# First two token tiles normalised as a pair in a state-space layer with a gated feed-forward block

## The chip, the cores and the metric

The kernel runs on one core of a Trainium2 chip. The metric is the device time of one execution in microseconds (us); the median over several executions counts. A core has five engines that run side by side: TensorE (PE, with its weight loads PEld) does matrix products and transposes into PSUM, VectorE (DVE) and ScalarE (ACT) do elementwise work, GpSimd (POOL) small things, and SyncE (SP) issues most of the DMA transfers. ScalarE issues a few transfers as well.

## The reference

One input x of 2048 tokens by 512 features is normalised over its features (no scale or shift). The normalised x goes through two branches, and both are added to x.

```python
def _layernorm(x, axis=-1, eps=1e-5):
    m = jnp.mean(x, axis=axis, keepdims=True)
    v = jnp.var(x, axis=axis, keepdims=True)
    return (x - m) / jnp.sqrt(v + eps)

# branch A: a diagonal complex state-space layer, 512 states
Lam_bar = jnp.exp(dt * Lam)
B_bar = ((Lam_bar - 1.0) / Lam)[:, None] * Bmat
Bu = jnp.einsum("bld,pd->blp", x + 0j, B_bar)
for t in range(L):
    h = Lam_bar[None, :] * h + Bu[:, t, :]
y = 2.0 * jnp.einsum("blp,dp->bld", hseq, Cmat).real + x * Dskip[None, None, :]

# branch B: feed-forward with 1376 hidden columns
(_gelu(x @ w_gate) * (x @ w_up)) @ w_down

xn = _layernorm(x)
return x + _A_ref(xn, ...) + _B_ref(xn, ...)
```

## The kernel before

The 2048 tokens are four blocks of 512, and each block is four tiles of 128 tokens. For each block b: `LN(b)` normalises the tiles, a transpose puts features on the partitions (`XNT[b]`), `GU` does the gate and up products with GELU and the product of both, `BU` the product with B, `CHAIN` the rotation and the scans of the state-space layer on VectorE, and `DN` the down product together with the product with C, after which the result is stored. Weights stay in SBUF.

The program is a list of operations with their reads and writes. `Sched.schedule` (line 128) plans an order for each engine from durations that are written out by hand: six rounds of a forward and a backward pass, of which the shortest plan is kept. TensorE and SyncE keep the order in which the program names their operations; VectorE, ScalarE and POOL are ordered by the plan. `emit` (line 283) then adds a wait on a semaphore wherever one engine needs another's result. The argument `after` of an operation is an additional condition on the order.

The change touches the start of the program, where TensorE has no normalised tokens yet. The order of TensorE's work there is given by lines 906 to 913:

- Ten matmuls on zeros of 512 columns ("warm", line 896) run while the data is on its way.
- Tile 0 goes alone through `LN` (line 598) with `halves=True`: statistics (line 604) and their aggregation (605) on VectorE, a cast of the mean on POOL (606), the addition of eps on VectorE (608), the root on ScalarE (609), the reciprocal (616) and the normalisation in two halves of 256 columns (622) on VectorE.
- `TR0(0, "AV")` transposes the halves of tile 0 on TensorE (line 647) into two PSUM banks. ScalarE copies the first half to SBUF (654), VectorE the second (656).
- `fill(3)`: three further matmuls on zeros, of 128 columns (line 902).
- Tile 1 goes alone through `LN`. Its statistics are held until tile 0's eps addition, its aggregation until tile 0's normalisation, by `GATE["bnag"]` and `GATE["xn"]`. Its eps addition (611) and root (612) are on ScalarE. Tiles 2 and 3 go as a pair, also with 611 and 612, held until tile 1 is normalised.
- `GU_first` (line 725) starts the gate and up products of block 0 with three column groups of 128 for tile 0 alone (line 736; 24 matmuls of 128 columns). After 16 of them `TR0(1, "A")` (line 755) transposes tile 1, and ScalarE copies it. `params()` transposes the parameters of the state-space layer (line 538); VectorE copies them (540) and computes small things with them (559, 560, 542). Then the same groups for tile 1 (24 matmuls), four matmuls of 256 columns for both tiles, the transposes of tiles 2 and 3 (`TR0(2, "V")`, `TR0(3, "A")`), and matmuls of 256 columns for the rest.
- The evacuations with GELU on ScalarE (744, 746) come after the copy of tile 3; `tables_dve` (587, 589) come after the copy of tile 2.

The loads of x are four transfers of 128 KB (line 472) on SyncE's queue; the weights follow in chunks (line 468): the first gate chunk on ScalarE's queue, then the first up chunk and the second gate and up chunks on SyncE's. After them SyncE issues block 1 of x (462) and the transposing loads of B (490).

Of the kernel before, what the change touches and what calls it, by code (L numbers as in the profile page):

```python
# [9 lines left out]
ALU = mybir.AluOpType  # L10
ACTF = mybir.ActivationFunctionType
BF16, F32, I32 = dt.bfloat16, dt.float32, dt.int32
# [334 lines left out]
NT, NB, KD, KP, KF = 16, 4, 4, 4, 11  # L347
# [4 lines left out]
EPS_BF16 = 1.0013580322265625e-05  # L352
# [12 lines left out]
def build(nc, ins, out):  # L365
    with ExitStack() as es:
# [47 lines left out]
                       buf.ap[:, b, j0:j1])  # L414
        XTk = [[Buf("XT%d_%d" % (b, i), "xt", 4 * b + i, 4 * b + i + 1) for i in range(4)] for b in range(NB)]
        XT0 = XTk[0]
        XT0h = [Buf("XT0_0h%d" % i, "xt", 0.5 * i, 0.5 * (i + 1)) for i in range(2)]
        XNh = [Buf("XN0h%d" % i, "sb", XN[0].lo + 512 * i, XN[0].lo + 512 * (i + 1)) for i in range(2)]
        XTr = lambda b: XTk[b]
        WRM = A.alloc("WRM", [128], BF16)  # L420
        PROW = A.alloc("PROW", [128], BF16)
# [173 lines left out]
            t = ACT(lambda e: e.activation(COST.ap, A1.ap, ACTF.Sin, bias=HPI.ap, scale=-SIN_SCALE), d_act(2048), [A1, HPI], [COST], "cost", after=[t])  # L595
            return ACT(lambda e: e.activation(SINT.ap, F1.ap, ACTF.Sin, scale=-SIN_SCALE), d_act(2048), [F1], [SINT], "sint", after=[t])  # L596

        def LN(b, js=range(4), on_act=False, after=(), halves=False):
            j0, j1 = js[0], js[-1] + 1
            mn, sbq, qb, rq = (cols(t, b, j0, j1) for t in (MN, SBQ, QB, RQ))  # L600
            mv = Buf("MV%d_%d" % (b, j0), "sb", MVt[b][j0].lo, MVt[b][j1 - 1].hi, MV[b].ap[:, j0:j1])
            for j in js:
                tt = 4 * b + j
                V(lambda e, tt=tt: e.bn_stats(ST[tt].ap, X[tt].ap), d_dve_1x(512), [X[tt]], [ST[tt]], "bnst", after[:1])  # L604
                GATE["bnag"] = V(lambda e, tt=tt, j=j: e.bn_aggr(MVt[b][j].ap, ST[tt].ap), D_TINY, [ST[tt]], [MVt[b][j]], "bnag", after[1:])
            POOL(lambda e: e.tensor_copy(mn.ap, mv.ap[:, :, 0]), 200, [mv], [mn], "mn")
            if halves:
                GATE["bnag"] = V(lambda e: e.tensor_scalar(sbq.ap, mv.ap[:, :, 1], EPS_BF16, None, ALU.add), D_TINY, [mv], [sbq], "sbq")
                ACT(lambda e: e.activation(qb.ap, sbq.ap, ACTF.Sqrt), d_act(4), [sbq, SCR], [qb], "sqrt")
            elif on_act:  # L610
                ACT(lambda e: e.activation(sbq.ap, mv.ap[:, :, 1], ACTF.Identity, bias=EPS.ap), d_act(4), [mv, EPS, SCR], [sbq], "sbq")
                ACT(lambda e: e.activation(qb.ap, sbq.ap, ACTF.Sqrt), d_act(4), [sbq], [qb], "sqrt")
            else:
                V(lambda e: e.tensor_scalar(sbq.ap, mv.ap[:, :, 1], EPS_BF16, None, ALU.add), D_TINY, [mv], [sbq], "sbq")
                POOL(lambda e: e.tensor_tensor(qb.ap, sbq.ap, HALF.ap[:, 0:j1 - j0], ALU.pow), 1100, [sbq, HALF], [qb], "pow")
            V(lambda e: e.reciprocal(rq.ap, qb.ap), 150, [qb], [rq], "rq")
            for j in js:
                tt = 4 * b + j
                xs = XN[tt % 8]
                for c0, c1 in (((0, 256), (256, 512)) if halves else ((0, 512),)):  # L620
                    w = [XNh[c0 // 256]] if halves else [xs]
                    GATE["xn"] = V(lambda e, tt=tt, j=j, xs=xs, c0=c0, c1=c1: e.tensor_scalar(  # L622
                        xs.ap[:, c0:c1], X[tt].ap[:, c0:c1], mn.ap[:, j - j0:j - j0 + 1], rq.ap[:, j - j0:j - j0 + 1],
                        ALU.subtract, ALU.mult), 190 + 0.13 * (c1 - c0) if halves else d_dve_ts4x(512), [X[tt], mn, rq], w, "ln_n",
                                   [GATE["xn"]] if c0 else ())

        def SKIP(b):
            for tt in range(4 * b, 4 * b + 4):
# [3 lines left out]

        TBANK = []

        def TR0(j, engs):
            if not TBANK:
                TBANK.extend([next_bank(), next_bank()])
            per = KD // len(engs)
            for n, eng in enumerate(engs):
                bank = TBANK[(j + n) % 2]  # L640
                pt = PS[bank].bitcast(BF16)

                def f(e, n=n, pt=pt):
                    ins_ = None
                    for q in range(per):
                        k = per * n + q
                        ins_ = e.transpose(pt[:, 128 * q:128 * (q + 1)], XN[j].ap[:, 128 * k:128 * (k + 1)], IDN.ap)
                    return ins_
                PE(f, 75.0 * per, [XN[j] if len(engs) == 1 else XNh[n], IDN], [BANK[bank]], "T0")
                dst = XNT[0].ap[:, per * n:per * (n + 1), 128 * j:128 * (j + 1)]  # L650
                src = pt[:, 0:128 * per].rearrange("p (q t) -> p q t", q=per)
                tok = XT0[j] if len(engs) == 1 else XT0h[n]
                if eng == "A":
                    GATE["evTA"] = ACT(lambda e, src=src, dst=dst: e.activation(dst, src, ACTF.Copy), d_act(128 * per), [BANK[bank]], [tok], "evT")
                else:
                    GATE["evT"] = V(lambda e, src=src, dst=dst: e.tensor_copy(dst, src), 110 + 0.6 * 128 * per, [BANK[bank]], [tok], "evT")  # L656

        def TR(b):
            tts = list(range(4 * b, 4 * b + 4))
# [62 lines left out]
            V(lambda e: e.tensor_tensor(ssb.ap[:, :, 1, :], TB.ap[:, :, 0, :], TA.ap[:, :, 1, :], ALU.subtract),  # L722
              d_dve_tt2x(2048), [TA, TB], [SSc[k3][s][1] for s in range(KP)], "post_im")

        def GU_first(fts, early, single):
            banks = [{ft: next_bank() for ft in fts} for h in range(2)]

            def mm(ft, u, j0, j1):
                W, Wc = ((WG, WGc), (WU, WUc))[u]
                h, q0 = j0 // 2, 256 * u + 128 * (j0 % 2)  # L730
                bank = banks[h][ft]

                def f(e):
                    ins_ = None
                    for dk in range(KD):
                        ins_ = e.matmul(PS[bank][:, q0:q0 + 128 * (j1 - j0)], W.ap[:, dk, 128 * ft:128 * (ft + 1)],  # L736
                                        XNT[0].ap[:, dk, 128 * j0:128 * j1], start=(dk == 0), stop=(dk == KD - 1))
# [12 lines left out]

            for u in range(2):
                for ft in early:
                    mm(ft, u, 0, 1)
                    if single and u == 1 and ft == early[0]:
                        TR0(1, "A")
            params()
            for ft in early:
                for u in range(2):
                    mm(ft, u, 1, 2)
            late = [ft for ft in fts if ft not in early]  # L760
            mm(late[0], 0, 0, 2)
            TR0(2, "V")
            TR0(3, "A")
            for ft in early:
                evac(ft, 0, [GATE["evTA"]])
            for ft in late[1:]:
                mm(ft, 0, 0, 2)
            for ft in late:
                mm(ft, 1, 0, 2)
                evac(ft, 0)  # L770
            for ft in fts:
                for u in range(2):
                    mm(ft, u, 2, 4)
                evac(ft, 1)
# [111 lines left out]
                    for c in parts:  # L886
                        hidden(j, *c); states(j, *c); store(j, *c)

        nwarm = 10
        wrm4 = WRM.ap.unsqueeze(1).broadcast_to([128, 4, 128])  # L890
        wb = next_bank()

# [5 lines left out]
        def fill(n):  # L898
            def f(e):
                ins_ = None  # L900
                for _ in range(n):
                    ins_ = e.matmul(PS[wb][:, 0:128], WRM.ap, WRM.ap, start=True, stop=True)
                return ins_
            PE(f, 60.0 * n, [WRM], [BANK[wb]], "fill")

        PE(fwarm, d_pe([512] * nwarm) * 1.6, [WRM], [BANK[wb]], "warm")
        LN(0, [0], True, halves=True)
        TR0(0, "AV")
        fill(3)
        LN(0, [1], True, [GATE["bnag"], GATE["xn"]])  # L910
        LN(0, [2, 3], True, [GATE["xn"]])
        load_B()
        GU_first(range(5), range(3), True)
        tables_dve()
        GATE["before_gelu"] = [tables_act([GATE["last_gelu"]])]
        BU(0)
# [81 lines left out]
```

## Time and profile before

| | us |
|---|---|
| median of 4 runs | 179.85 |
| lowest and highest | 179.81 and 180.42 |
| the profiled execution | 179.85 |
| its span, first to last instruction | 178.0 |
| TensorE busy | 173.6 |
| VectorE busy | 157.8 |
| ScalarE busy | 92.3 |
| POOL busy | 10.2 |

Times in the profile are counted from the start of the span. A row of a timeline is a run of like instructions of one engine: start, length until the last one ends, engine, line of the kernel, operation, result and operand, the number of instructions, and in brackets the idle time of the engine before it with what ended it. Instructions of one engine overlap in part, so that a row can reach beyond the start of the next; the ends of matmuls are modelled.

### The profile page before, as it was taken

The numbers are of one execution on the slowest core, as the hardware profiler recorded it, in microseconds if no ns is written. First come the engines' busy times: TensorE is split into PE (matmuls) and PEld (weight loads), VectorE is DVE, ScalarE is ACT, GpSimd is POOL, SyncE is SP. The second block draws the span as 40 slices with busy tenths as digits, with TensorE's granted clock in tenths as the row PEclk, the third lists the DMA queues.
The fourth block names the chain that finished last, engine by engine and source line by source line (L and its number), as shares of the span: only waits on it lengthen the run. The fifth ranks groups of instructions, "written<-read, shape, count | busy, mean of one in ns | idle before, by whom it ended". The sixth has DMA issues, their size and how long they took to land.

```text
span 178.0 us, 2528 instructions
## 1 busy us (share of the span) xinstructions
PE 173.6 (97%) x914; PEld 86.6 (49%) x929; DVE 157.8 (89%) x277; ACT 92.3 (52%) x179; POOL 10.2 (6%) x21
## 2 busy tenths in 40 slices
PE   7999999999999999999999999999999999999994
PEld 2597464444644444444644444444464444444453
DVE  4869998997998989989999999989999999999511
ACT  3389999976677799002667793000667800710000
POOL 3020022042000000200000000000000000000000
PEclk9999999999999999999999999999999999999999
DMA  5999914989045000002014100000001000002211
GB/s 132 344 294 169 312 37 90 152 224 327 1 88 63 0 0 0 2 29 92 0 29 89 30 0 4 29 29 29 29 4 29 0 0 0 0 0 66 85 49 40
DMA packets 26387, 12.90 MB, mean 72 GB/s; under 512 B 17704, under 2 KB 26376, under 8 KB 26376
## 3 DMA queue, kind: packets, MB, share of 16 engines
q1 hardware_dynamic: 25824, 12.36, 28.5%
q10 hardware_dynamic: 552, 0.40, 0.9%
q8 instruction: 7, 0.11, 0.3%
q14 instruction: 4, 0.03, 0.1%
HBM read 6.46 MB, written 2.10 MB: 48 GB/s over the span
## 4 chain that ended last, share of the span: by engine, by line
PE 83%; ACT 5%; DVE 2%; issue 1%; ACTq 0%
PE PS L853 37%; PE PS L813 33%; PE PS L673 12%; PE PS L787 2%; ACT arena L677 2%; ACT arena L595 1%; ACT arena L596 1%; DVE arena L748 1%; DVE arena L589 1%; ACT L594 1%; DVE arena L587 0%; ACT arena L746 0%; DVE arena L871 0%; ACT arena L744 0%; ACT arena L594 0%
## 5 line engine op out<-in xcount | busy, mean ns | idle before, releaser
L853 PE MATMUL PS<-arena 128*128 128x512 bf16 (+3 forms) x317 | 65.9, 366 | 0.3
L813 PE MATMUL PS<-arena 128*128 128x512 bf16 x273 | 60.7, 379 | 0.4
L853 PEld LDWEIGHTS PS<-arena 128*128 128x128 bf16 (+1 forms) x323 | 30.8, 98 | 35.2
L828 ACT ACTIVATE arena<-PS 128x512 bf16<-128x512 f32 x35 | 21.1, 603 | 46.8 <-PE PS L813 33.5
L813 PEld LDWEIGHTS PS<-arena 128*128 128x128 bf16 x280 | 27.4, 98 | 32.1
L706 DVE TENSOR_TENSOR_SCAN arena<-arena 128x512 bf16<-128x512 f32 x32 | 39.1, 1255 | 0.9 <-POOL arena L544 0.9
L673 PE MATMUL PS<-arena 128*128 128x512 bf16 x126 | 28.0, 379 | 0.1
L831 ACT ACTIVATE arena<-PS 128x512 bf16<-128x512 f32 x35 | 21.1, 603 | 5.2 <-PE PS L813 5.1
L673 PEld LDWEIGHTS PS<-arena 128*128 128x128 bf16 x128 | 12.5, 98 | 14.9
L677 ACT ACTIVATE arena<-PS 128x512 bf16<-128x512 f32 x32 | 18.0, 597 | 2.2 <-PE PS L673 2.2
L871 DVE TENSOR_TENSOR arena<-PS,arena 128x512 bf16<-128x512 f32 (+2 forms) x17 | 10.9, 652 | 9.0 <-PE PS L853 8.9
L833 DVE TENSOR_TENSOR arena<-arena 128x512 bf16<-128x512 bf16 x35 | 13.7, 414 | 2.1 <-ACT arena L831 2.0
L845 ACT ACTIVATE PS<-arena 128x512 f32<-128x512 bf16 (+2 forms) x17 | 9.6, 581 | 5.8 <-DVE arena L871 5.1
L604 DVE BATCH_NORM_STATS2 arena<-arena 128x6 f32<-128x512 bf16 x16 | 10.3, 683 | 1.4 <-DMA arena<-in_A_x_dram 1.2
L736 PE MATMUL PS<-arena 128*128 128x256 bf16 (+1 forms) x104 | 9.5, 248 | 0.4 <-DVE arena L656 0.3
L693 DVE TENSOR_TENSOR arena<-arena 128x4096 bf16<-128x4096 bf16 (+1 forms) x5 | 9.3, 1856 | 0.0
L695 DVE TENSOR_TENSOR arena<-arena 128x4096 bf16<-128x4096 bf16 (+1 forms) x5 | 9.3, 1856 | 0.0
L718 DVE TENSOR_TENSOR arena<-arena 128x4096 bf16<-128x4096 bf16 x4 | 9.2, 2288 | 0.1
L719 DVE TENSOR_TENSOR arena<-arena 128x4096 bf16<-128x4096 bf16 x4 | 9.1, 2283 | 0.0
L736 PEld LDWEIGHTS PS<-arena 128*128 128x128 bf16 x104 | 8.1, 98 | 1.3 <-issue 0.5
L622 DVE TENSOR_SCALAR arena<-arena 128x512 bf16<-128x512 bf16 (+1 forms) x17 | 6.1, 401 | 0.4
L787 PE MATMUL PS<-arena 128*128 128x192 bf16 x64 | 5.9, 246 | 0.0
(89 smaller groups left out, 108.4 us busy)
## 6 DMA issues: line engine op xcount, KB each, us to landing
out_dram<-arena SPq DMA_DIRECT2D x15, 128.0 KB, 1.7
arena<-in_A_x_dram SPq DMA_DIRECT2D x3, 512.0 KB, 6.9
arena<-in_B_w_down_dram SPq DMA_DIRECT2D x1, 1280.0 KB, 6.5
arena<-in_A_x_dram SPq DMA_DIRECT2D x4, 128.0 KB, 2.9
arena<-in_B_w_gate_dram SPq DMA_DIRECT2D x1, 512.0 KB, 6.1
arena<-in_B_w_up_dram SPq DMA_DIRECT2D x1, 512.0 KB, 7.0
arena<-in_B_w_gate_dram SPq DMA_DIRECT2D x1, 480.0 KB, 4.2
arena<-in_B_w_up_dram SPq DMA_DIRECT2D x1, 480.0 KB, 5.9
```

What stands on the lines that cost most here:

```text
L604: V(lambda e, tt=tt: e.bn_stats(ST[tt].ap, X[tt].ap), d_dve_1x(512), [X[tt]], [ST[tt]], "bnst", after[:1])
L673: ins_ = e.matmul(PS[bank][:, :], BBT[c][dk].ap[:, 128 * s:128 * (s + 1)], XNT[b].ap[:, dk, :], start=(dk == 0), stop=(dk == KD - 1))
L677: ACT(lambda e, bank=bank, k3=k3, s=s, c=c: e.activation(SSc[k3][s][c].ap, PS[bank][:, :], ACTF.Copy), d_act(512), [BANK[bank]], [SSc[k3][ ...
L706: V(lambda e, g=g, rb=rb, init=init: e.tensor_tensor_scan(g.ap, rb, g.ap, init, ALU.mult, ALU.add), d_dve_scan(512), [g, PA[RRr]] + ([CARc ...
L736: ins_ = e.matmul(PS[bank][:, q0:q0 + 128 * (j1 - j0)], W.ap[:, dk, 128 * ft:128 * (ft + 1)], XNT[0].ap[:, dk, 128 * j0:128 * j1], start=( ...
L813: ins_ = e.matmul(PS[bank][0:m, c0:c1], W.ap[:, dk, 128 * ft:128 * ft + m], XNT[b].ap[:, dk, c0:c1], start=(dk == 0), stop=(dk == KD - 1))
L828: GATE["last_gelu"] = ACT(lambda e, bg=bg, kk=kk, m=m: e.activation(GG[kk].ap[0:m, :], PS[bg][0:m, :], ACTF.Gelu_apprx_tanh), d_act(512), ...
L831: ACT(lambda e, bu=bu, kk=kk, m=m: e.activation(UPB[kk].ap[0:m, :], PS[bu][0:m, :], ACTF.Copy), d_act(512), [BANK[bu]], [UPB[kk]], "evU")
L833: V(lambda e, kk=kk, m=m, ft=ft, k2=k2: e.tensor_tensor(HTt[k2][ft].ap[0:m, :], GG[kk].ap[0:m, :], UPB[kk].ap[0:m, :], ALU.mult), d_dve_tt ...
L845: ACT(lambda e: e.activation(PS[bank][:, c0:c1], X[tt].ap[:, c0:c1], ACTF.Copy), d_act(c1 - c0), [X[tt]], [BANK[bank]], "seed")
L853: ins_ = e.matmul(PS[bank][:, c0:c1], l_[:, 128 * j:128 * (j + 1)], r_[:, c0:c1], start=False, stop=last and n == len(ops) - 1, skip_group ...
L871: V(lambda e: e.tensor_tensor(OUTB[ko].ap[:, c0:c1], PS[bank][:, c0:c1], XD[tt].ap[:, c0:c1], ALU.add), d_dve_1x(c1 - c0), [BANK[bank], XD ...
```

## The change

Tiles 0 and 1 now go through `LN` together, in the way in which tiles 2 and 3 did: both statistics, both aggregations, one cast of the means, one eps addition, one root and one reciprocal for two columns, and then the normalisation of each tile in one instruction of 512 columns. The eps addition is on VectorE for every group (line 611 on ScalarE is gone). `TR0` transposes a whole tile into one bank, with one copy: tile 0's on VectorE, tile 1's on ScalarE. Both are transposed ahead of the first product, and the transposes of tile 1 between the products of tile 0 are gone. The conditions that held tile 1's statistics and aggregation are gone; those of tiles 2 and 3 are held until VectorE's copy of tile 0. There are eleven instead of ten warm-up matmuls and two instead of three fills. The modelled durations of the transposes and copies are other numbers too.

```diff
-        def LN(b, js=range(4), on_act=False, after=(), halves=False):
+        def LN(b, js=range(4), on_act=False, after=()):
...
-                V(lambda e, tt=tt: e.bn_stats(ST[tt].ap, X[tt].ap), d_dve_1x(512), [X[tt]], [ST[tt]], "bnst", after[:1])
-                GATE["bnag"] = V(lambda e, tt=tt, j=j: e.bn_aggr(MVt[b][j].ap, ST[tt].ap), D_TINY, [ST[tt]], [MVt[b][j]], "bnag", after[1:])
+                V(lambda e, tt=tt: e.bn_stats(ST[tt].ap, X[tt].ap), d_dve_1x(512), [X[tt]], [ST[tt]], "bnst", after)
+                V(lambda e, tt=tt, j=j: e.bn_aggr(MVt[b][j].ap, ST[tt].ap), D_TINY, [ST[tt]], [MVt[b][j]], "bnag")
             POOL(lambda e: e.tensor_copy(mn.ap, mv.ap[:, :, 0]), 200, [mv], [mn], "mn")
-            if halves:
-                GATE["bnag"] = V(lambda e: e.tensor_scalar(sbq.ap, mv.ap[:, :, 1], EPS_BF16, None, ALU.add), D_TINY, [mv], [sbq], "sbq")
+            V(lambda e: e.tensor_scalar(sbq.ap, mv.ap[:, :, 1], EPS_BF16, None, ALU.add), D_TINY, [mv], [sbq], "sbq")
+            if on_act:
                 ACT(lambda e: e.activation(qb.ap, sbq.ap, ACTF.Sqrt), d_act(4), [sbq, SCR], [qb], "sqrt")
-            elif on_act:
-                ACT(lambda e: e.activation(sbq.ap, mv.ap[:, :, 1], ACTF.Identity, bias=EPS.ap), d_act(4), [mv, EPS, SCR], [sbq], "sbq")
-                ACT(lambda e: e.activation(qb.ap, sbq.ap, ACTF.Sqrt), d_act(4), [sbq], [qb], "sqrt")
             else:
-                V(lambda e: e.tensor_scalar(sbq.ap, mv.ap[:, :, 1], EPS_BF16, None, ALU.add), D_TINY, [mv], [sbq], "sbq")
                 POOL(lambda e: e.tensor_tensor(qb.ap, sbq.ap, HALF.ap[:, 0:j1 - j0], ALU.pow), 1100, [sbq, HALF], [qb], "pow")
...
-                for c0, c1 in (((0, 256), (256, 512)) if halves else ((0, 512),)):
-                    w = [XNh[c0 // 256]] if halves else [xs]
-                    GATE["xn"] = V(lambda e, tt=tt, j=j, xs=xs, c0=c0, c1=c1: e.tensor_scalar(
...
+                V(lambda e, tt=tt, j=j, xs=xs: e.tensor_scalar(
+                    xs.ap, X[tt].ap, mn.ap[:, j - j0:j - j0 + 1], rq.ap[:, j - j0:j - j0 + 1], ALU.subtract, ALU.mult),
+                  d_dve_ts4x(512), [X[tt], mn, rq], [xs], "ln_n")
...
-        def TR0(j, engs):
+        def TR0(j, eng):
             if not TBANK:
                 TBANK.extend([next_bank(), next_bank()])
...
+            bank = TBANK[j % 2]
+            pt = PS[bank].bitcast(BF16)
+
+            def f(e):
+                ins_ = None
+                for q in range(KD):
+                    ins_ = e.transpose(pt[:, 128 * q:128 * (q + 1)], XN[j].ap[:, 128 * q:128 * (q + 1)], IDN.ap)
+                return ins_
+            PE(f, 56.0 * KD, [XN[j], IDN], [BANK[bank]], "T0")
+            dst = XNT[0].ap[:, :, 128 * j:128 * (j + 1)]
+            src = pt[:, 0:512].rearrange("p (q t) -> p q t", q=KD)
+            if eng == "A":
+                GATE["evTA"] = ACT(lambda e: e.activation(dst, src, ACTF.Copy), d_act(512), [BANK[bank]], [XT0[j]], "evT")
+            else:
+                GATE["evT"] = V(lambda e: e.tensor_copy(dst, src), 420, [BANK[bank]], [XT0[j]], "evT")
...
             for u in range(2):
                 for ft in early:
                     mm(ft, u, 0, 1)
-                    if single and u == 1 and ft == early[0]:
-                        TR0(1, "A")
             params()
...
-        nwarm = 10
+        nwarm = 11
...
-        LN(0, [0], True, halves=True)
-        TR0(0, "AV")
-        fill(3)
-        LN(0, [1], True, [GATE["bnag"], GATE["xn"]])
-        LN(0, [2, 3], True, [GATE["xn"]])
+        LN(0, [0, 1], True)
+        TR0(0, "V")
+        TR0(1, "A")
+        fill(2)
+        LN(0, [2, 3], True, [GATE["evT"]])
         load_B()
-        GU_first(range(5), range(3), True)
+        GU_first(range(5), range(3))
```

More of the change, by code (lines that the diff above doesn't have):

```diff
@@ L416, in build @@
         XT0 = XTk[0]
-        XT0h = [Buf("XT0_0h%d" % i, "xt", 0.5 * i, 0.5 * (i + 1)) for i in range(2)]
-        XNh = [Buf("XN0h%d" % i, "sb", XN[0].lo + 512 * i, XN[0].lo + 512 * (i + 1)) for i in range(2)]
         XTr = lambda b: XTk[b]
@@ L619, in LN @@
                 xs = XN[tt % 8]
-                for c0, c1 in (((0, 256), (256, 512)) if halves else ((0, 512),)):
-                    w = [XNh[c0 // 256]] if halves else [xs]
[L622 to L625, printed above, removed]
+                V(lambda e, tt=tt, j=j, xs=xs: e.tensor_scalar(
+                    xs.ap, X[tt].ap, mn.ap[:, j - j0:j - j0 + 1], rq.ap[:, j - j0:j - j0 + 1], ALU.subtract, ALU.mult),
+                  d_dve_ts4x(512), [X[tt], mn, rq], [xs], "ln_n")
         def SKIP(b):
@@ L633, in build @@
         TBANK = []
-        def TR0(j, engs):
+        def TR0(j, eng):
             if not TBANK:
                 TBANK.extend([next_bank(), next_bank()])
[L638 to L656, printed above, removed]
+            bank = TBANK[j % 2]
[12 more added lines that the diff above has]
+                GATE["evT"] = V(lambda e: e.tensor_copy(dst, src), 420, [BANK[bank]], [XT0[j]], "evT")
         def TR(b):
@@ L723, in CHAIN, with GU_first @@
               d_dve_tt2x(2048), [TA, TB], [SSc[k3][s][1] for s in range(KP)], "post_im")
-        def GU_first(fts, early, single):
+        def GU_first(fts, early):
             banks = [{ft: next_bank() for ft in fts} for h in range(2)]
```

## The prediction

> **What bounds the kernel now.** I read the page first: engine shares, then the timeline of each engine over the first 17 us, then the chain of waits and the landings of the loads.
>
> ```profile
> PE 173.6 (97%) x914; PEld 86.6 (49%) x929; DVE 157.8 (89%) x277; ACT 92.3 (52%) x179; POOL 10.2 (6%) x21
> ```
>
> TensorE (PE) is busy for 97% of the span. The share is an average, so the question is where its idle stretches lie. Its timeline (start, length, engine, line, count, idle before):
>
> ```profile
> 0.99 4.45 PE L896 MATMUL PS<-arena 128*128 128x512 bf16 x10 [0.99 <-DVE arena L516]
> 5.41 0.67 PE L647 MATMUL PS<-arena 128*128 128x128 bf16 x4
> ...
> 6.55 1.12 PE L736 MATMUL PS<-arena 128*128 128x128 bf16 x16 [0.31 <-DVE arena L656]
> 7.51 0.39 PE L647 MATMUL PS<-arena 128*128 128x128 bf16 x4
> 7.74 0.61 PE L736 MATMUL PS<-arena 128*128 128x128 bf16 x8
> 8.28 0.18 PE L538 MATMUL PS<-arena 12*128 12x12 bf16 x1
> 8.59 1.95 PE L736 MATMUL PS<-arena 128*128 128x128 bf16 x28
> 10.38 0.65 PE L647 MATMUL PS<-arena 128*128 128x128 bf16 x8
> 10.87 5.84 PE L736 MATMUL PS<-arena 128*128 128x256 bf16 x52
> ```
>
> From 8.59 on each group starts where the one before runs out, and the chain of waits is then nearly all TensorE, back to back to 175.8 us. So whatever moves the start of the 256-column matmuls (10.87) moves the end by the same amount, as long as no other engine becomes late. Ahead of it TensorE waits for the layer norm of the first tiles, on VectorE (DVE) and ScalarE (ACT):
>
> ```profile
> 2.93 0.69 DVE L604 BATCH_NORM_STATS2 arena<-arena 128x6 f32<-128x512 bf16 x1 [1.20 <-DMA arena<-in_A_x_dram]
> 3.66 0.18 DVE L605 BATCH_NORM_AGGREGATE arena<-arena 128x2 bf16<-128x6 f32 x1
> 3.87 0.16 DVE L608 TENSOR_SCALAR arena<-arena 128x1 bf16<-128x1 bf16 x1
> ...
> 5.00 0.73 DVE L622 TENSOR_SCALAR arena<-arena 128x256 bf16<-128x256 bf16 x2
> ...
> 6.11 0.29 DVE L656 COPY arena<-PS 128x256 bf16<-128x256 bf16 x1 [0.16 <-PE PS L647]
> 6.68 0.16 DVE L616 RECIPROCAL arena<-arena 128x1 f32<-128x1 bf16 x1 [0.27 <-ACT arena L612]
> 6.95 0.41 DVE L622 TENSOR_SCALAR arena<-arena 128x512 bf16<-128x512 bf16 x1
> 7.46 1.29 DVE L604 BATCH_NORM_STATS2 arena<-arena 128x6 f32<-128x512 bf16 x2
> 8.67 0.30 DVE L605 BATCH_NORM_AGGREGATE arena<-arena 128x2 bf16<-128x6 f32 x2
> ```
> ```profile
> 4.13 0.20 ACT L609 ACTIVATE arena<-arena 128x1 bf16<-128x1 bf16 x1
> 7.94 0.60 ACT L654 ACTIVATE arena<-PS 128x512 bf16<-128x512 bf16 x1 [1.29 <-PE PS L647]
> 9.00 0.29 ACT L611 ACTIVATE arena<-arena 128x2 bf16<-128x2 bf16 x1 [0.47 <-DVE arena L540]
> ```
>
> The reader is to see two waits. The first matmul (6.55) comes 0.15 us after VectorE's copy ends at 6.40. The tile-1 matmuls (8.59) come 0.05 us after ScalarE's copy of tile 1 ends at 8.54; the row of TensorE waits gives that one 0.2 us.
>
> **The change, step by step, until the first matmul.** Each offset is a difference of rows above. Statistics of tile 0 start at 2.93 as now (the loads of x are untouched). Those of tile 1 follow 0.60 later (1.29 - 0.69, from the pair at 7.46): 3.53; its data lands at about 3.4 (issue 1.2, 2.2 to landing). Aggregates: the pair at 7.46 reaches them 1.21 later, so 4.14; two take 0.30, end 4.44. The eps addition on VectorE starts 0.03 later: 4.47. Root: 0.26 after that start (3.87 to 4.13): 4.73; ScalarE is free, its first root ended at 3.99. Reciprocal 0.24 later (6.44 to 6.68): 4.97. Normalisation 0.27 later: 5.24; one whole tile 0.41, so 5.65. Transpose of tile 0: 0.06 after (5.35 to 5.41): 5.71. The eleventh warm-up matmul adds 0.43 and runs out at about 5.66, just clear of it. A whole transposed tile reaches its copy 0.42 after its first transpose (10.38 to 10.80). I add 0.05, because the warm-up runs at 0.43 us per 512 columns while later matmuls take 0.216: TensorE is at half pace until about 5.8, in the middle of these transposes. Copy on VectorE from 6.18, 0.42 for 512 columns (the row at 10.80): 6.60. First matmul 0.05 to 0.15 later, by the two waits above; I take the middle, **6.70, 0.15 later than now**. That is what the halves were worth.
>
> **From there to 10.87.** Now 6.55 to 8.59 is 2.04 us: 24 matmuls at 0.056 (24 of 128 columns and 4 of 256 take 1.79 from 8.59 to 10.38; four at 0.109 leave 1.35), that is 1.34; four transposes 0.22; the other 0.48 is the parameter transpose and waits, the one on tile 1's copy foremost. Afterwards tile 1 is transposed ahead of the first matmul (normalised 5.57 to 5.98, copied by ScalarE 0.60 from about 6.46 to 7.06), so its transposes and its wait are both gone from this stretch: 6.70 + 1.34 = 8.04; parameter transpose 0.15 (0.09 gap as now at 8.19 to 8.28, and 0.06); 8.19 + 1.79 = 9.98 for the transposes of tile 2, now 10.38. **Shift: -0.40 us.** A fill fewer (0.056) lies in idle time before the first matmul.
>
> Tiles 2 and 3 must be ready by 9.98. Their statistics are held until the copy of tile 0 ends (6.60); by the offsets above normalisation starts 2.31 after the statistics: 6.64 + 2.31 = 8.95, ended 9.36, at most 0.3 more if the parameter operations (0.13, 0.18, 0.15) fall between: 9.7, still 0.25 ahead. The tile-1 matmuls until 9.98 are the work that hides this chain; whatever of it goes beyond is paid in full. The new condition (statistics of tile 2 after tile 0's copy) makes VectorE wait for no other engine, as the copy is its own; queued behind are the parameter copies, which only the tables after 11 us need. ScalarE loses two eps additions (0.29 each) and one root (0.20), POOL one cast (0.19), VectorE one reciprocal (0.16): all in idle time of those engines, costed at nothing. No DMA moves on any queue, SP's and POOL's included.
>
> What TensorE meets sooner: the up weights for tile 0 land at 7.24 (2.64 + 4.6), wanted at 7.37; the second gate chunk at 9.22 (3.12 + 6.1), wanted 9.53; the second up chunk at 10.67 (3.67 + 7.0), wanted at about 10.9; the transposed B at 15.4 (4.87 + 10.5), wanted near 16.1. All fit, the up chunk with 0.2 to spare. ScalarE's copy of tile 3 (11.07), its GELU table load (11.68) and the evacuations follow the same transposes, so they move along.
>
> Bounds. Upper: if tile 0's aggregate goes before tile 1's statistics, 0.2 more; with 0.05 for the handoff the shift is -0.15. Lower: handoff 0.05 and no half pace, -0.5.
>
> **A rule on the clock.** The row shows the pace doubling between 4.80 and 5.8. The Trainium skill ("TensorE: Matmul & The Clock Gate", Part 1: The HAM clock gate) says the clock is released after a window of some 3.4 us of activity that runs free of the kernel, so the point varies by about half a microsecond from run to run. By the row the sum is -0.40; by a release half a microsecond later, at 6.3, an estimate from that page's figure is some 0.2 us less gain, as only the transposes would be slow.
>
> **The sum.** The profiled execution took 179.85 us (span 178.0 and 1.85 around it), equal to the median of the runs. 179.85 - 0.40 = 179.45, with 179.35 to 179.70 from the bounds.
>
> **Rivals.**
> (1) *A transfer takes the shift back.* The second up chunk has 0.2 us to spare. For: it is the tightest landing, and this is one execution. Against: its issue at 3.67 depends on nothing that moves. If it lands 0.2 to 0.4 later than in the trace, 0 to 0.2 of the shift is lost at first and all of it at 0.6: 179.65 to 179.85.
> (2) *Slower: the order is planned anew and VectorE becomes late at the end.* The planner orders VectorE and ScalarE for the whole kernel from its own durations. VectorE is 99% busy from 120 to 160 us (39.71 of 40) and ends the last chain at 160.4; TensorE wants it after 142.7 + 76 x 0.216 + 11 x 0.216 = 161.5. That is 1.1 us of slack, and one badly placed operation costs that order already: VectorE waits 0.90 us for POOL at 41.2. The point is 1.1 us of new VectorE idle; two more such waits, 1.8, make TensorE wait 0.7, three 1.6: with the shift, 180.15 to 181.05, middle 180.6. Against: in the planner's durations tile 1's matmuls start at the same place in both, so little below them has cause to move.
> (3) *The clock is released late.* Against: eleven warm-up matmuls keep TensorE as busy as before. Deciding point: each microsecond of half pace after 6.70 costs 0.5; slower than now from a release at 7.5, 180.1 at 8.0.
> (4) *More is gained.* TensorE has no idle left after 10.87 to win, so over 0.54 us needs the first matmul at or before 6.55: only with an unforeseen handoff.
>
> **Numbers.** A measurement of this kernel tells 0.3% (0.54 us) from no change: below 179.31 or above 180.39. Forecast 0.52; (1) 0.12; (2) 0.24; (3) 0.05; (4) 0.07. Faster takes (4) and 0.04 of the forecast: 0.11. Slower takes most of (2), some of (3), and 0.04 for orders that I can't see: 0.26. The same: 0.63. The range leaves out (4)'s far end and the upper part of (2): 179.1 to 180.6.
>
> **What would show it.** Right: first 128-column matmul near 6.70, no transposes between 6.7 and 8, no wait at the tile-1 matmuls, transposes of tile 2 near 9.98, 256-column matmuls near 10.47, and a stream without holes to about 175.4. Wrong: tile-2 transposes waiting for VectorE, the up weights at line 736 waiting for a DMA, or any TensorE gap over 0.3 us after 11 us, above all at line 853 near 161.

## The result and the profile after

The changed kernel takes 179.58 us (median of 33 runs, 179.36 to 180.02); the kernel before 179.84 (median of 53 runs, 179.66 to 180.42). The ratio is 0.9986 with a 95% interval of 0.9981 to 0.9991: a gain of 0.14%, real but inside the 0.3% that the prediction called no change. The forecast was 179.45 us, a shift of -0.40.

The profiled execution of the changed kernel took 180.25 us, 0.67 above the median. Where these 0.67 us went is also what the change is about. First the engine shares, then VectorE's timeline (start, length, engine, line, operation, count, idle before it):

```profile
PE 172.7 (97%) x914; PEld 86.5 (48%) x929; DVE 156.7 (88%) x276; ACT 92.0 (52%) x175; POOL 10.0 (6%) x20
```
```profile
2.92 0.69 DVE L602 BATCH_NORM_STATS2 arena<-arena 128x6 f32<-128x512 bf16 x1 [1.22 <-DMA arena<-in_A_x_dram]
4.04 0.69 DVE L602 BATCH_NORM_STATS2 arena<-arena 128x6 f32<-128x512 bf16 x1 [0.43 <-DMA arena<-in_A_x_dram]
4.65 0.30 DVE L603 BATCH_NORM_AGGREGATE arena<-arena 128x2 bf16<-128x6 f32 x2
4.99 0.17 DVE L605 TENSOR_SCALAR arena<-arena 128x2 bf16<-128x2 bf16 x1
...
5.77 0.74 DVE L614 TENSOR_SCALAR arena<-arena 128x512 bf16<-128x512 bf16 x2
6.67 0.42 DVE L643 COPY arena<-PS 128x512 bf16<-128x512 bf16 x1 [0.17 <-PE PS L635]
```

The second statistics row waits 0.43 us for the load of x: tile 1 landed at 4.0 instead of 3.4, and the whole pair, tile 0 with it, is normalised that much later (5.77, forecast 5.24). TensorE in the same execution:

```profile
6.24 0.72 PE L635 MATMUL PS<-arena 128*128 128x128 bf16 x8 [1.42 <-DVE arena L614]
6.80 0.28 PE L887 MATMUL PS<-arena 128*128 128x128 bf16 x2
7.25 1.50 PE L723 MATMUL PS<-arena 128*128 128x128 bf16 x24 [0.17 <-DVE arena L643]
8.68 0.18 PE L536 MATMUL PS<-arena 12*128 12x12 bf16 x1
8.79 1.95 PE L723 MATMUL PS<-arena 128*128 128x128 bf16 x28
10.57 0.61 PE L635 MATMUL PS<-arena 128*128 128x128 bf16 x8
11.02 5.84 PE L723 MATMUL PS<-arena 128*128 128x256 bf16 x52
```

The wait that the change was to remove is gone: after the parameter transpose at 8.68 TensorE goes on at 8.79, where the kernel before, after its one at 8.28, went on only at 8.59. The first matmul comes at 7.25 instead of 6.55, the 256-column matmuls at 11.02 instead of 10.87. Later in this execution TensorE has one more hole, ahead of the first B product of block 1:

```profile
26.86 6.85 PE L798 MATMUL PS<-arena 128*128 128x512 bf16 x31
33.78 6.42 PE L660 MATMUL PS<-arena 128*128 128x512 bf16 x28
```

A matmul of 512 columns takes 0.216; the first of these starts at 26.65 by the pace (its record is missing), and 32 of them end at 33.56. So 0.22 us are lost. Two of the transposing transfers of block 1, issued at 27.7 and 29.0:

```profile
L648 SPq DMA_TRANSPOSE arena<-arena x2: 1264/1264/1265, 27.7 to 29.0; - x2
...
DMA to landing us min/median/max: 2.5/3.5/4.5
```

One took the usual 2.5 us, the other 4.5: issued at 29.0, it landed at about 33.5, just ahead of the matmul that needs it.

Two explanations lay open. Theory A: the start gains what was computed, and loses again what the input data lands late. Theory B: the planner has made a new order for VectorE and ScalarE over the whole kernel (the two kernels' lists differ from the parameter operations on), and this order makes the hole at 33.6 in every execution.

### The profile page after: what moved, and what is told of

Read it like the earlier page. It is cut to its first block, busy times and chain, and to the rows that moved or that the text cites. A ratio compares the mean times of both kernels' runs of the same rounds, so it can differ in the third digit from the quotient of the medians.

```text
span 178.4 us, 2519 instructions
## 1 busy us (share of the span) xinstructions
PE 172.7 (97%) x914; PEld 86.5 (48%) x929; DVE 156.7 (88%) x276; ACT 92.0 (52%) x175; POOL 10.0 (6%) x20
## 4 chain that ended last, share of the span: by engine, by line
PE 94%; DMA 2%; DVE 1%; issue 1%; SPq 0%; ACT 0%; DVEq 0%; ACTq 0%
PE PS L838 37%; PE PS L798 34%; PE PS L660 16%; PE PS L723 5%; PE PS L772 3%; DMA arena<-in_A_x_dram 2%; PE PS L635 0%; DVE arena L602 0%; DVE arena L643 0%; DVE arena L614 0%; SPq L470 0%; DVE arena L856 0%; DVE arena L603 0%; ACT arena L607 0%; DVE arena L605 0%
## 5 line engine op out<-in xcount | busy, mean ns | idle before, releaser
L813 ACT ACTIVATE arena<-PS 128x512 bf16<-128x512 f32 x35 | 20.9, 599 | 43.4 <-PE PS L798 33.1
L816 ACT ACTIVATE arena<-PS 128x512 bf16<-128x512 f32 x35 | 20.8, 598 | 5.6 <-PE PS L798 5.4
L664 ACT ACTIVATE arena<-PS 128x512 bf16<-128x512 f32 x32 | 17.9, 600 | 3.6 <-PE PS L660 3.5
L614 DVE TENSOR_SCALAR arena<-arena 128x512 bf16<-128x512 bf16 x16 | 5.7, 404 | 0.3
```

Of the source, the lines that this page charges most:

```text
L664: ACT(lambda e, bank=bank, k3=k3, s=s, c=c: e.activation(SSc[k3][s][c].ap, PS[bank][:, :], ACTF.Copy), d_act(512), [BANK[bank]], [SSc[k3][ ...
L813: GATE["last_gelu"] = ACT(lambda e, bg=bg, kk=kk, m=m: e.activation(GG[kk].ap[0:m, :], PS[bg][0:m, :], ACTF.Gelu_apprx_tanh), d_act(512), ...
L816: ACT(lambda e, bu=bu, kk=kk, m=m: e.activation(UPB[kk].ap[0:m, :], PS[bu][0:m, :], ACTF.Copy), d_act(512), [BANK[bu]], [UPB[kk]], "evU")
```

## Experiments

The ratio given with a time is that to the kernel before, run beside it on the same chip (its median was 179.78 to 179.82 us there), with its 95% interval; it is not always the quotient of the two medians.

Where the planner would have made yet another order, an explicit one is put in its place after planning, in this manner (the lists hold the numbers of the operations):

```diff
         S.schedule()
+        for e_, ids in ORDER.items():
...
+            S.order[e_] = [S.ops[i] for i in ids]
         S.emit()
```

### The changed kernel again: after_again and after_third

No edit.

> The changed kernel once more, for a second profiled execution. Its first one took 180.25 us where the median of its runs is 179.58; in it the statistics of tile 1 started at 4.04 (0.43 us of waiting for x) and TensorE had a hole of 0.22 us at 33.6 before the first B product of block 1. Theory A (landing): the front end gains 0.40 us when tile 1's data is there, and the pair pays one for one for what it lands later than 3.5; expected here: statistics of tile 1 at 3.53 to 4.05, the first 128-column matmul 3.2 us after that start, time near 179.45 plus the lateness. Theory B (order): the newly planned order of VectorE and ScalarE makes the hole at 33.6 in every execution and costs 0.15 to 0.22 us; expected: the hole again, and x on time.

> The changed kernel a third time, on the same chip as the three others, for the comparison and for one more profile of the landings. Theory A: each profile's start of the 256-column matmuls is 10.47 plus what tile 1 lands beyond 3.53 plus any wait for the up chunk, within 0.1; no hole near 33.6 unless a transposing transfer lands late; median 179.45 to 179.80.

Measured: 179.78 us (179.36 to 180.10), ratio 0.9994 (0.9984 to 1.0003), and 179.52 (179.42 to 180.07), ratio 0.9990 (0.9980 to 0.9999). The profile of after_third is the undisturbed case, VectorE and TensorE:

```profile
2.96 1.29 DVE L602 BATCH_NORM_STATS2 arena<-arena 128x6 f32<-128x512 bf16 x2 [1.26 <-DMA arena<-in_A_x_dram]
...
6.19 0.42 DVE L643 COPY arena<-PS 128x512 bf16<-128x512 bf16 x1 [0.17 <-PE PS L635]
```
```profile
6.76 1.51 PE L723 MATMUL PS<-arena 128*128 128x128 bf16 x24 [0.17 <-DVE arena L643]
8.20 0.18 PE L536 MATMUL PS<-arena 12*128 12x12 bf16 x1
8.31 1.95 PE L723 MATMUL PS<-arena 128*128 128x128 bf16 x28
10.10 0.61 PE L635 MATMUL PS<-arena 128*128 128x128 bf16 x8
10.54 1.69 PE L723 MATMUL PS<-arena 128*128 128x256 bf16 x14
```

Both tiles' statistics run in one go, the second from 3.56 (2.96 + 1.29 - 0.69); the first matmul is at 6.76 (forecast 6.70), tile 2's transposes at 10.10 (9.98), the 256-column matmuls at 10.54 (10.47). That execution took 179.52 us. In after_again the data of tile 1 was on time too, but not the first up chunk:

```profile
6.64 0.83 PE L723 MATMUL PS<-arena 128*128 128x128 bf16 x12 [0.17 <-DVE arena L643]
7.89 0.84 PE L723 MATMUL PS<-arena 128*128 128x128 bf16 x12 [0.41 <-DMA arena<-in_B_w_up_dram]
...
11.01 1.26 PE L723 MATMUL PS<-arena 128*128 128x256 bf16 x10
```

The gate matmuls (12 at 0.056) are through at 7.31 and the next starts at 7.89: 0.58 us lost, the gain of the change and more, and the execution took 179.99. In neither profile is there a hole near 33.6. The hole that theory B took for a constant one was there in one execution, with one late transfer.

### Start and order taken apart: old_order and new_order

The changed kernel's start with the rest in the order of the kernel before, and the reverse; the lists are joined at the parameter copy on VectorE, the first evacuation on ScalarE and the exponential on POOL.

> The changed kernel's start, but from the parameter copy on VectorE, the first evacuation on ScalarE and the exponential on POOL the order in which the kernel before has them. Theory A (landing): like the changed kernel, 179.58 within 0.1. Theory B (order): the hole at 33.6 goes, 179.36 to 179.43.

> The reverse: the kernel before with its own start, and from the same places on the order that the changed kernel has. Theory A (landing): like the kernel before, 179.84 within 0.1. Theory B (order): 0.15 to 0.22 slower than it, 180.0 to 180.06, with a hole near 33.4.

Measured: old_order 179.65 us, ratio 0.9985 (0.9976 to 0.9993); new_order 179.84, ratio 1.0002 (0.9991 to 1.0013). So the start carries the difference, with the old order as with the new (0.9994 for after_again on the same chip; the intervals overlap). That the new order costs nothing doesn't follow from the median of new_order, whose interval reaches up to 0.23 us; it follows from the profiles. That of new_order has no hole near 34.3, where its first B product of block 1 stands, and from the start of the 256-column matmuls on both orders take the same time within 0.05 us (see the sums below). So theory B falls. One thing is left of it: the four transposing transfers of block 1 begin 14.0 to 14.5 us after the first 256-column matmul with the new order (eleven profiles), and 13.8 after it with the old one (three). A late transfer has less room there, and in the first execution the order may have had a share in the hole.

Two rows of old_order's TensorE show the start once more with a tile 1 that is a quarter of a microsecond late (statistics at 3.78):

```profile
6.99 1.50 PE L753 MATMUL PS<-arena 128*128 128x128 bf16 x24 [0.17 <-DVE arena L673]
...
10.76 0.49 PE L753 MATMUL PS<-arena 128*128 128x256 bf16 x3
```

The profiled execution of new_order took 180.75 us. It shows that the old start is open to late weights as well:

```profile
7.12 0.84 PE L766 MATMUL PS<-arena 128*128 128x128 bf16 x12 [0.83 <-DMA arena<-in_B_w_gate_dram]
8.21 0.40 PE L766 MATMUL PS<-arena 128*128 128x128 bf16 x4 [0.25 <-DMA arena<-in_B_w_up_dram]
```

### One part undone: t1_middle

```diff
                 for ft in early:
                     mm(ft, u, 0, 1)
+                    if u == 1 and ft == early[0]:
+                        TR0(1, "A")
...
         TR0(0, "V")
-        TR0(1, "A")
         fill(2)
```

> The changed kernel with one part undone: tile 1 is transposed after 16 of tile 0's matmuls, as before, with the changed kernel's order on the other engines. By the prediction's steps the first matmul stays at 6.70, the transposes of tile 1 come at 7.60, ScalarE's copy ends at 8.62, the tile-1 matmuls start at 8.67 and the transposes of tile 2 at 10.46: 0.08 behind the kernel before, 179.9. So the pair by itself costs a little, and moving the transposes of tile 1 is what gains. If the gain came from the pair or the eps addition instead, it would stay near 179.6.

Measured: 180.08 us (179.84 to 180.33), ratio 1.0004 (0.9994 to 1.0015). The gain is gone, as expected: the pair with its whole tiles doesn't gain by itself, the place of tile 1's transposes does. TensorE:

```profile
6.88 1.05 PE L753 MATMUL PS<-arena 128*128 128x128 bf16 x16 [0.50 <-DVE arena L673]
7.78 0.39 PE L665 MATMUL PS<-arena 128*128 128x128 bf16 x4
8.00 0.61 PE L753 MATMUL PS<-arena 128*128 128x128 bf16 x8
8.54 0.18 PE L566 MATMUL PS<-arena 12*128 12x12 bf16 x1
8.85 1.95 PE L753 MATMUL PS<-arena 128*128 128x128 bf16 x28
...
11.08 0.38 PE L753 MATMUL PS<-arena 128*128 128x256 bf16 x2
```

The transposes stand among tile 0's products again, and so does the wait for their copy (8.54 to 8.85, where after_third goes from 8.20 to 8.31). From the first matmul to the 256-column ones it takes 4.20 us, in after_third 3.78. Tile 1's statistics started at 3.63 in this execution; without these 0.10 us the 256-column matmuls would stand at 10.98, 0.11 behind the kernel before, where 0.08 was expected. The eleventh warm-up matmul, the fill and the eps addition were not undone one by one; this run has them all as in the changed kernel and gains nothing.

### Landings moved: x1_first, gate_later, x1_third and x1_third_before

x1_first gives tile 1's load the first place on ScalarE's queue (the gate chunk second):

```diff
-            S.dma(lambda e, j=j: e.dma_start(X[j].ap, ...), 128 * 1024, writes=[X[j]], tag="ld_x0")
+            S.dma(lambda e, j=j: e.dma_start(X[j].ap, ...), 128 * 1024, writes=[X[j]], tag="ld_x0", queue="scalar" if j == 1 else "sync")
```

> The changed kernel in its own order, with tile 1's load as the first one on ScalarE's queue (0.74 instead of 1.17 on SyncE's), and the first gate chunk right behind it. Theory A (landing): tile 1 is there by 3.5 in nearly all executions, statistics of tile 1 at 3.53, first 128-column matmul near 6.7, median 179.43 to 179.50 and a narrower spread. Theory B (order): like the changed kernel, 179.58, with the hole at 33.6.

Measured: 179.91 us (179.72 to 180.00), ratio 1.0002 (0.9993 to 1.0011). A miss, and an instructive one. VectorE's first rows:

```profile
3.34 1.28 DVE L636 BATCH_NORM_STATS2 arena<-arena 128x6 f32<-128x512 bf16 x2 [1.64 <-DMA arena<-in_A_x_dram]
```

Tile 1 landed at 3.5 as wanted, but tile 0, loading at the same moment, came at 3.3 instead of 2.9. The statistics of tile 1 then follow at 3.93, and the first matmul at 7.13. The spread is narrow and the gain is lost: both theories failed on the median, and A only by its guess that tile 0 would not mind.

gate_later issues the first gate chunk after the three parameter loads on ScalarE's queue (an edit of the order alone).

> The changed kernel in its own order, with the first gate chunk issued on ScalarE's queue after all three parameter loads, about 0.4 us later. Theory A (landing, in the form the last runs left): what lands beside x sets when tile 1's last piece comes (3.42 to 4.16 in five profiles, the gate chunk issued at 1.59); with the gate chunk out of the way tile 1 lands by 3.5, median 179.45 to 179.50. The gate chunk itself then lands near 6.1, wanted at 6.7. If the lateness of tile 1 has nothing to do with the gate chunk: like the changed kernel, 179.58 to 179.78.

Measured: 180.06 us (179.62 to 180.50), ratio 1.0007 (0.9996 to 1.0019). Also a miss: in its profile the statistics of tile 1 start at 3.61, so this one profile gives no sign that the gate chunk makes tile 1 late, though it can't rule it out. The up chunk was late in it, as in after_again:

```profile
7.92 0.84 PE L753 MATMUL PS<-arena 128*128 128x128 bf16 x12 [0.27 <-DMA arena<-in_B_w_up_dram]
```

Whether the later gate chunk makes the up chunk late more often isn't shown by one profile; a median of 180.06 and a lowest time of 179.62 would fit it.

What makes the last piece of tile 1 late in some executions stays open. That its lateness is paid was tried directly, by exchanging the loads of tile 1 and tile 2 in both kernels (the edit in words; it stands in the explicit order of SyncE):

```diff
-SyncE: x tile 0, x tile 1, x tile 2, x tile 3, ...
+SyncE: x tile 0, x tile 2, x tile 1, x tile 3, ...
```

> The changed kernel in its own order with the loads of tile 1 and tile 2 in exchanged places on SyncE's queue, so that tile 1 lands where tile 2 did, at L = 5.3 to 5.8. Theory A (landing): the pair pays every microsecond beyond 3.53, that is L - 3.53; at L = 5.5 it is 179.45 + 1.97 = 181.4, slower than the kernel before with the same exchange (next run) by 0.2. If the pair did not hang on tile 1's landing: below 180.

> The kernel before in its own order with the same exchange. Tile 1's statistics stand ahead of tile 0's reciprocal in VectorE's order, but start only at 4.14, so it pays what tile 1 lands beyond that, L - 4.14; at L = 5.5: 179.85 + 1.36 = 181.2. So the sign of the change flips: here the kernel before is ahead by 0.2. If the change's gain has nothing to do with the landing, the changed kernel stays ahead by 0.2 to 0.4.

Measured: 183.57 us (ratio 1.0200, 1.0178 to 1.0223) for the changed start and 181.70 (1.0103, 1.0074 to 1.0133) for the old one. The statistics of tile 1 start at 5.54 and 5.57 in the two profiles, so the landing is the same in both, and the sign of the change flips as expected. But the changed start is behind by 1.87 instead of 0.2. In x1_third the rows of TensorE say why:

```profile
8.95 2.72 PE L757 MATMUL PS<-arena 128*128 128x128 bf16 x24
11.60 0.19 PE L570 MATMUL PS<-arena 12*128 12x12 bf16 x1
11.72 2.95 PE L757 MATMUL PS<-arena 128*128 128x128 bf16 x28
...
14.95 1.25 PE L757 MATMUL PS<-arena 128*128 128x256 bf16 x10
```

24 matmuls take 2.72 us instead of 1.50: 0.107 each, half pace. The next 28 take 2.95 instead of 1.95. The first matmul at 8.95 is 0.2 later than the 8.74 that the statistics at 5.54 give (5.54 + 3.20, see the sums below), as tile 0's transposes ran at half pace too, and half pace, until about 13.9 by the spacing of the matmuls, costs the rest. The kernel before lost less to the clock (see the last section). So most of the 1.87 us is the clock's, and the flip of the medians alone wouldn't prove the landing. The rows do:

```profile
5.57 0.69 DVE L638 BATCH_NORM_STATS2 arena<-arena 128x6 f32<-128x512 bf16 x1 [1.53 <-DMA arena<-in_A_x_dram]
```
```profile
7.98 1.86 PE L770 MATMUL PS<-arena 128*128 128x128 bf16 x16 [0.31 <-DVE arena L690]
```

In x1_third_before the first product comes 2.41 us after tile 1's statistics, as in the kernel before (4.14 to 6.55); in x1_third 3.41 after them, 3.20 and the slow transposes. Each start pays what tile 1 lands late, from 4.14 and from 3.53 on.

### The clock: no_warm

```diff
-        nwarm = 11
+        nwarm = 1
```

> The changed kernel in its own order with one warm-up matmul instead of eleven. This prices the third rival, the clock of TensorE: if the pace rises only after some 3.4 to 4.8 us of activity, which then starts at 5.7, the first stretch runs at half pace until 9 to 10.5 and the kernel takes 1.3 to 2.0 us longer, 180.9 to 181.6, with tile-0 matmuls 0.107 apart. If the pace does not depend on the warm-up: like the changed kernel, 179.6.

Measured: 181.14 us (180.81 to 181.93), ratio 1.0077 (1.0050 to 1.0104). The data was on time; what is slow is TensorE:

```profile
6.95 2.57 PE L753 MATMUL PS<-arena 128*128 128x128 bf16 x24
9.56 1.95 PE L753 MATMUL PS<-arena 128*128 128x128 bf16 x28
...
11.80 1.47 PE L753 MATMUL PS<-arena 128*128 128x256 bf16 x12
```

Tile 0's products run at 0.107, and from 9.23 on, by the trace's clock record, at full pace (28 in 1.95 again). Half pace has the price that was expected for it. The change doesn't call it up: the eight profiles with ten or eleven warm-up matmuls and x's loads in their place that have a clock record show the release of the clock between 4.2 and 6.0, ahead of the first product. Three others with eleven warm-up matmuls have no record, and there the spacing of the matmuls has to tell: full pace from about 3.7 in after and x1_first, but only from about 6.7 in gate_first.

### Versions that may beat both: gate_first and split_copy

gate_first wants the up chunk 0.7 us later by doing the gate products of both tiles first:

```diff
             for u in range(2):
                 for ft in early:
                     mm(ft, u, 0, 1)
-            params()
-            for ft in early:
-                for u in range(2):
+                if u == 0:
+                    params()
+                for ft in early:
                     mm(ft, u, 1, 2)
```

> The changed kernel in its own order on the other engines, but TensorE does the gate products of tile 0 and tile 1 before the up products, so that the first up chunk is wanted at about 8.2 instead of 7.4. Theory A (landing): late up weights (7.84 in one profile, 0.41 us of waiting) no longer cost anything; the slow part of the distribution near 180.0 thins out, median 179.45 to 179.60 depending on tile 1's landing. If the up chunk is late too seldom to matter: like the changed kernel.

Measured: 179.61 us (179.40 to 180.71), ratio 0.9985 (0.9971 to 1.0000): like the changed kernel. Its profile had tile 1 late (statistics at 3.69) and the transposes of tiles 0 and 1 at half pace (8 in 0.97 instead of 0.72), so that the first product came 3.42 after the statistics instead of 3.20. Whether it spares the executions with a late up chunk can't be told from 12 runs.

split_copy adds to it that tile 0's transposed tile is copied half by ScalarE, half by VectorE:

```diff
-        TR0(0, "V")
+        TR0(0, "AV")
...
+                    if n == 0:
+                        ACT(lambda e, hd=hd, hs=hs: e.activation(hd, hs, ACTF.Copy), ...)
+                    else:
+                        GATE["evT"] = V(lambda e, hd=hd, hs=hs: e.tensor_copy(hd, hs), ...)
...
-            bank = TBANK[j % 2]
+            bank = 7 if j == 1 else TBANK[j % 2]
```

> A version that may beat both: the pair as changed, the gate products of both tiles ahead of the up products, and tile 0's transposed tile copied in two halves by ScalarE and VectorE (tile 1 in another bank). The first matmul comes about 0.13 us sooner (a copy of 0.29 instead of 0.42), and a late up chunk is not waited for: 179.30 to 179.45 by theory A; if the input loads set the pace already, like the changed kernel, 179.6.

Measured: 179.46 us (179.26 to 180.03), ratio 0.9982 (0.9974 to 0.9991). It is faster than the kernel before, and its 179.26 is the lowest time of all; against the changed kernel on the same chip (179.52) the intervals overlap. Its first matmul and its 256-column matmuls:

```profile
6.70 0.83 PE L771 MATMUL PS<-arena 128*128 128x128 bf16 x12
...
10.47 5.73 PE L771 MATMUL PS<-arena 128*128 128x256 bf16 x51
```

The statistics of tile 1 started at 3.64 here, so the first matmul came 3.06 after them instead of 3.20: the split copy is worth 0.14, as computed.

### The sums

From the timelines: the start of tile 1's statistics, of the first 128-column product, of the 256-column products, and the time of that execution.

| profile | statistics | first product | 256 columns | time | time - 256 columns |
|---|---|---|---|---|---|
| before | 4.14 | 6.55 | 10.87 | 179.85 | 168.98 |
| after (first) | 4.04 | 7.25 | 11.02 | 180.25 | 169.23 |
| after_again | 3.44 | 6.64 | 11.01 | 179.99 | 168.98 |
| after_third | 3.56 | 6.76 | 10.54 | 179.52 | 168.98 |
| old_order | 3.78 | 6.99 | 10.76 | 179.77 | 169.01 |
| new_order | 4.19 | 7.12 | 11.76 | 180.75 | 168.99 |
| t1_middle | 3.63 | 6.88 | 11.08 | 180.10 | 169.02 |
| x1_first | 3.93 | 7.13 | 10.91 | 179.94 | 169.03 |
| gate_later | 3.61 | 6.82 | 11.04 | 180.02 | 168.98 |
| gate_first | 3.69 | 7.11 | 10.89 | 179.91 | 169.02 |
| split_copy | 3.64 | 6.70 | 10.47 | 179.46 | 168.99 |
| no_warm | 3.53 | 6.95 | 11.80 | 180.81 | 169.01 |
| x1_third | 5.54 | 8.95 | 14.95 | 183.94 | 168.99 |
| x1_third_before | 5.57 | 7.98 | 13.39 | 182.38 | 168.99 |

The last column is 168.98 to 169.03 in all but one, over 4.5 us of different starts; the exception is the execution with the late transposing transfer. Everything that these kernels differ in happens in the first 15 us. In six profiles with the changed start (after, after_again, after_third, old_order, x1_first, gate_later) the first product is 3.20 or 3.21 after tile 1's statistics; in gate_first, no_warm and x1_third, with the transposes at half pace, it is 3.41 or 3.42.

In the first four of the six, taking off what the statistics start beyond 3.53, and the 0.58 for the up chunk, the 256-column products stand at 10.51, 10.52, 10.51 and 10.51: the change with punctual data is worth 10.87 - 10.51 = 0.36 us. Of this 0.26 is left in the medians. The difference is about what tile 1 is late: in the nine profiles with the changed start and x's loads in their place its statistics start at 3.44 to 4.04, the middle one at 3.63, 0.10 beyond 3.53. Nine executions give that only roughly, and late up chunks come on top.

## Why the prediction was right, point by point

- **The first matmul at 6.70, 0.15 later.** Right: 6.76 with tile 1's statistics at 3.56; 3.17 after these were forecast, 3.20 measured. In part two errors cancel here: in after_third the clock was released at 4.78, ahead of the transposes, so that the 0.05 added for half pace wasn't spent, and the handoff from the copy (6.19 + 0.42 = 6.61) to the first product took 0.15, not the 0.10 taken. Where the transposes did run at half pace, in gate_first, it cost 0.21.
- **The stretch to the 256-column matmuls is 0.55 shorter** (3.83 to 3.28 up to tile 2's transposes). Right: 3.83 to 3.34 in after_third (6.76 to 10.10), and another 0.05 in the transposes of tiles 2 and 3 (0.49 to 0.44), which no longer wait for tile 3: 0.54 in all. t1_middle shows that it comes from the place of tile 1's transposes.
- **Tiles 2 and 3 ready in time.** Right; nothing in these profiles waits for them. In after_third their normalisation starts at 8.96, forecast 8.95.
- **What TensorE meets sooner.** Here the working was too sure. It took the landings of one execution as given, tile 1 at 3.4 and the up chunk at 7.24, and called them met with 0.1. (For the up chunk it speaks of 0.2 to spare, but its own 7.24 and 7.37 leave 0.13.) In other profiles tile 1's statistics had to wait until 3.78, 4.04 or 4.19, and the up chunk until 7.9 or 8.2. The bounds contained neither. The term of the sum that was too small is this lateness, set at nothing and about 0.10 us in the middle profile: the pair has moved the point from which tile 1's landing is paid from 4.14 to 3.53. It fits what lies between 179.45 and the median: 56 runs of the changed kernel have their median at 179.61, 28 of them lie between 179.36 and 179.60, and 13 above 179.80. The undisturbed profile is at 179.52. So the forecast of 179.45 holds for an execution with punctual data, within 0.07, and not for the median.
- **Rival 1, the up chunk takes the shift back.** It did so in one of three profiles of the changed kernel, where the up weights waited for a DMA, which the prediction had named as a sign of being wrong: it belongs in the spread, not beside the forecast as another case.
- **Rival 2, a new order with VectorE late at the end.** The planner did make a new order, against the argument that little had cause to move; new_order and the sums show that it costs nothing that these runs can tell. VectorE does wait for POOL twice in after_third, 1.8 us in all where it was 0.9 once, but TensorE has no new hole for it; the prediction had counted on 1.1 us of slack.
- **Rival 3, the clock.** Not called up by the change. The trace has the release at 5.82 in the kernel before, and at 4.37 and 4.78 in two profiles of the changed one. The Trainium skill ("TensorE: Matmul & The Clock Gate", Part 1: The HAM clock gate) speaks of a window that runs free of the kernel and of a spread of half a microsecond to either side. Over these profiles the release lies between 4.2 and 6.0, and from about 3.7 to 6.7 with the three that show it only by the spacing, so more than that. It is early enough in all but gate_first, where the slow transposes cost 0.2, the size that the prediction had estimated for a late release.
- **Rival 4, more than 0.54.** No run's median comes near; the lowest single time of the changed kernel, 179.36, is 0.48 below the old median.

## What to carry to other kernels

Look for the one point behind which the bounding engine never stops again: when every profile has the same time from there to the end (169.0 us here), an experiment is judged by where that point lies, here to 0.05 us from one profile, where medians need dozens of runs. What one profile can't give is the spread of what comes before that point. A wait that is removed at such a start is gained only until the next input is late; a price that hangs on a DMA landing should be taken from several profiles, as a spread. Joining two tiles makes the first as late as the second one's data, and it pays here because the transposes of the second tile leave the stretch that counts.

## What was not expected

The granted clock can fall after a pause of 2 us. In x1_third_before the trace gives, by stretches of the span (length, then busy time of PE, PEld, DVE, ACT and POOL with their counts, granted clock, DMA share, GB/s):

```profile
5.00:6.00 1.00, 0.00 (x0) 0.00 (x0) 0.43 (x1) 0.00 (x0) 0.00 (x0) 1.00 1.09 373
6.00:7.00 1.00, 0.17 (x2) 0.11 (x2) 0.86 (x4) 0.00 (x0) 0.00 (x0) 1.00 1.07 324
7.00:8.00 1.00, 0.60 (x8) 0.34 (x7) 0.63 (x3) 0.81 (x3) 0.19 (x1) 0.79 1.01 290
8.00:9.00 1.00, 1.00 (x11) 1.00 (x12) 0.75 (x3) 0.01 (x1) 0.00 (x0) 0.50 1.06 372
...
11.00:12.00 1.00, 1.00 (x18) 0.93 (x17) 0.59 (x5) 0.47 (x3) 0.41 (x1) 1.00 1.35 157
```

The clock was released at 4.16; TensorE then stood still for about 2 us, until 6.83, and at 7.57 the clock went to half for 3.41 us, while TensorE was already at work again. So a pause of 2 us ahead of the first products is paid twice, once as the pause and again by the half pace behind it: the 256-column products start at 13.39, where the 10.87 of the kernel before and statistics that are 1.43 later give 12.30.

The six runs of this kernel fall into two groups, 180.86 to 181.08 and 182.31 to 182.38. The mean granted clock of each run tells them apart: 0.991 in the three slower ones, which is what 3.41 us at half pace make of a span of 180.6 us, and 1.000 in the three others. So in all six the slower time and the fall of the clock go together. Why the clock fell in three of them and not in the others isn't shown; only one of the six has a timeline. (A mean of 1.000 says that no fall is on record, and not that the pace was full from the start: no_warm has it too.)
